# Retention chunks tiled across the batches, integer passes in PSUM, one weight load later

## The chip, the cores and the metric

The kernel runs on one core of one Trainium2 chip. The metric is device time in microseconds (us), the median of three runs. The profile is one execution of its own, read with the chip's hardware profiler.

## The reference

Three layers follow one another; all inputs are float32 but the dense layer's weights `w_in` and `w_out`, which are float64.

```python
# 1. retention: q, k, v of 4 batches x 8 heads x 576 x 64
scores = scale * np.matmul(q, k.transpose(0, 1, 3, 2))
Dmat = np.where(rel >= 0, gamma[:, None, None] ** rel[None, :, :], 0.0)
x = np.matmul(scores * Dmat[None], v)            # then laid out as 2304 tokens x 512
# 2. dense layer, 512 -> 2048 -> 512
h = x @ w_in
x = (np.maximum(h, 0.0) + np.log1p(np.exp(-np.abs(h)))) @ w_out
# 3. routed layer: 8 experts, the best two of each token
noisy = x @ w_gate + np.log1p(np.exp(x @ w_noise)) * noise
for e in range(E):
    for k in range(2):
        h = np.maximum(x[mask] @ w1[e], 0.0)
        out[mask] += top2_w[mask, k, None] * (h @ w2[e])
```

## The kernel before

**Retention** is done in chunks of 96 positions, six to a sequence, 24 in all. A chunk's own part is a masked product: Q is the product of its k and q (`att_qk`, L218), multiplied by the mask on VectorE (L222), and V is that times v (`att_av`, L258). What comes from earlier chunks of the same sequence goes through a state: K sums the scaled k times v (`att_kv`, L235) onto the last state (L238), and a later chunk adds state times scaled q to its V (L254). S scales q and k on GpSimd (`att_scale`, L206 and L209). Chunks are numbered batch by batch, so the first chunk of a sequence, which needs no state, is every sixth, and a tile of four chunks (384 tokens) holds four neighbours in one sequence. ScalarE and VectorE write a chunk's result as a high and a low float16 half (L264, L265).

**The dense layer** goes tile by tile, six tiles of 16 steps. A step is twelve products of the first layer (`g1`, L277), its relu and absolute value on ScalarE (L286, L287), the exp and ln for two steps together (L289, L290), a sum and a cast on VectorE (L291, L292), the low half on GpSimd for the first 24 steps (L294), and four steps later nine products of the second layer (`g2`, L308). High and low halves are multiplied three ways.

**Decoding.** The float64 weights of this layer come as 16 pieces of 1 MB, loaded in the order of a list (i: first layer, o: second). Each is turned into float32 by ScalarE and VectorE (`decode`, L135 to L140), and then into a high half on ScalarE (L146) and a low one on GpSimd (L147). Piece i0 serves the first two steps, i1 the next two, and so on. The third layer's weights are float32 and are split in the same way in 64 units, stored to DRAM (L321 to L335).

**The order of the work** at the beginning is a table, `START`: A loads a chunk, S, Q, K, V as above, L loads a piece, a decodes one, b splits it, g is a step, r loads what the router needs, W is warming of TensorE. From there on `at` hooks chunks and units to steps. A scheduler then sets the order on each engine from this and from its own estimates. Every engine, and the DMA queue on SyncE (SP), works its own list in order; the instruction at its head may wait for a semaphore and holds up those behind. Buffers are shared: two arrays `w1` and `w2` (in the traces w, in the orders below w_84 and w_85) hold first the pieces and all that belongs to retention, later the experts' weights. A ring with n places makes its n+1st writer wait for the first reader. Products L218, L235 and L258 share two PSUM tiles (pa), the first layer has two (pg), the second three (p2, also used by the first chunks), and a last bank (sm) serves the router.

**The routed layer** needs a schedule of blocks, made by VectorE in two parts, the first before the last tile is through. Then 41 blocks follow: a gather on GpSimd, a transpose by DMA (L621), the first product (L633), a transpose, the second product (L650), and an addition into the output. `weights(i, half)` loads 2 MB of an expert's weights, half 0 for the first product and half 1 for the second; `out_zero` writes zeros to the output beforehand (L350). The last tile's router waits for its own transposed rows (L394, L406).

Of the kernel before, what the change touches and what calls it, by code (L numbers as in the profile page):

```python
# [45 lines left out]
def consts():  # L46

    gamma = 1.0 - 2.0 ** (-5.0 - np.arange(H))
    i = np.arange(C)
    rel = i[None, :] - i[:, None]  # L50
    m = np.where(rel >= 0, gamma[:, None, None] ** np.maximum(rel, 0), 0.0) / np.sqrt(D)
    g = gamma.reshape(4, 2).T
    s = np.arange(S)
    cq = np.repeat(g[:, None, :, None] ** s, D, axis=1) / np.sqrt(D)
    ck = gamma[None, :] ** -s[:, None]
    return {
        "c_m": m.reshape(4, 2, C, C).transpose(2, 1, 0, 3).astype(np.float32),
        "c_q": cq.reshape(P, 4, NCB, C).transpose(2, 0, 1, 3).astype(np.float32),
        "c_k": ck.reshape(NCB, C, H).transpose(1, 0, 2).astype(np.float32),
    }  # L60


def chunks(q, k, v):


    def cols(a):
        return a.reshape(B, 4, 2, NCB, C, D).transpose(0, 3, 2, 5, 1, 4).reshape(B * NCB, P, 4, C)

    def rows(a):
        return a.reshape(B, H, NCB, C, D).transpose(0, 2, 3, 1, 4).reshape(B * NCB, C, H, D)  # L70

    return {"qk": np.stack([cols(q), cols(k)], axis=2), "kv": np.stack([rows(k), rows(v)], axis=2)}
# [3 lines left out]
def body(ctx, tc, ins, out):  # L76
# [49 lines left out]
    def decode(d):  # L126
# [10 lines left out]
        nc.scalar.activation(w[:, :, 0], u[:, :, 1], AF.Copy, bias=2.0 ** -14 - 0.5, scale=2.0 ** -13)  # L137
        nc.vector.scalar_tensor_tensor(out=A, in0=w[:, :, 1], scalar=3, in1=w[:, :, 0],
                                       op0=ALU.logical_shift_left, op1=ALU.bitwise_or)
        nc.vector.scalar_tensor_tensor(out=A, in0=w[:, :, 1], scalar=-2 ** 31, in1=A,  # L140
                                       op0=ALU.bitwise_and, op1=ALU.bitwise_or)
# [37 lines left out]

    cm = view(1, 12288, [2, 4 * C], F32, C).rearrange("p a (b c) -> p a b c", b=4)  # L180
# [3 lines left out]
    def att_load(c):  # L184
        cc = c % NCB
# [4 lines left out]
        kv = ap.tile([C, 2, H, D], F32, name="kv", bufs=3)  # L190
        nc.sync.dma_start(out=kv, in_=ins["kv"][c])
        if c == 0:
            nc.sync.dma_start(out=ck, in_=ins["c_k"])
        if 0 < c < NCB:
            CQ[c] = view(1, 15616 + (c - 1) * 1536, [4, C], F32)
            nc.sync.dma_start(out=CQ[c], in_=ins["c_q"][c])
        LD[c] = (qk, kv)

    def att_scale(c):
        qk, kv = LD[c]  # L200
        cc = c % NCB
        qs = ks = None
        e = nc.vector if c < 1 else nc.gpsimd
        if cc < NCB - 1:
            ks = ring("ks", 1, 23296, [H, D], F32, 2, C)
            e.tensor_tensor(out=ks, in0=kv[:, 0], in1=ck[:, cc, :, None].to_broadcast([C, H, D]), op=ALU.mult)  # L206
        if cc:
            qs = ring("qs", 1, 27392, [4, C], F32, 2)
            e.tensor_tensor(out=qs, in0=qk[:, 0], in1=CQ[cc], op=ALU.mult)  # L209
        SC[c] = (qs, ks)  # L210

    def att_qk(c):

        qk, kv = LD[c]
        pa = [ps1.tile([C, 4, C], F32, tag="pa", name="pa", bufs=2) for g in range(2)]
# [9 lines left out]
    def att_kv(c, tag="pa"):  # L225
        (qk, kv), (qs, ks) = LD[c], SC[c]
        cc = c % NCB
        if cc == NCB - 1:
            return
        pst = ps.tile([P, 4, D], F32, tag=tag, name="pst", bufs=3) if tag == "p2" else \  # L230
            ps1.tile([P, 4, D], F32, tag="pa", name="pst", bufs=2)

        for j in range(4):
            for r in range(2):
                nc.tensor.matmul(pst[ROW[r], j], lhsT=ks[:, 2 * j + r], rhs=kv[:, 1, 2 * j + r], start=True, stop=True)  # L235
        st = ring("st", 1, 30464, [4, D], F32, 2)
# [4 lines left out]
        ST[c + 1] = st  # L241

    def att_av(c, tag="pa"):
        (qk, kv), (qs, ks), a = LD.pop(c), SC.pop(c), AA.pop(c)
        cc = c % NCB
# [10 lines left out]
        for j in range(4):  # L256
            for r in range(2):
                nc.tensor.matmul(px[ROW[r], j, :], lhsT=kv[:, 1, 2 * j + r], rhs=a[r][:, j], start=n < 2, stop=n >= last - 1)  # L258
# [99 lines left out]
    def route_load():  # L358
        nc.sync.dma_start(out=table.rearrange("(p a c) f -> p a (c f)", p=P, c=17),
                          in_=init.rearrange("p (o c) f -> p o (c f)", o=1).to_broadcast([P, NCOL // 17, 68]))  # L360
        nc.sync.dma_start(out=noise, in_=ins["moe2_noise"].rearrange("(j p) e -> p j e", p=P))
# [12 lines left out]
    nc.gpsimd.iota(tok, pattern=[[P, NB]], base=0, channel_multiplier=1)  # L374
    ones = rt.tile([P, P], F16, name="ones")
# [64 lines left out]
    def ranks(t):  # L440
# [28 lines left out]
        nc.vector.tensor_copy(tb[:, :, :, 1], tkb)  # L469
# [249 lines left out]
    for n in range(64):  # L719
# [9 lines left out]
        W6 W16 A0 L A1 S0 Q0 K0 A2 L S1 V0 Q1 K1 A3 L a V1 S2 Q2 K2 L V2 S3 a b Q3 K3 L V3 a b L g g  # L729
        a A4 b L g g a S4 b L g Q4 a K4 b A5 L g g V4 a b L g S5 g Q5 a b L g K5 A6 g a V5 b L g g S6  # L730
        a b L g Q6 g a K6 b A7 L g V6 g a b S7 L g g Q7 a b K7 A8 L g V7 g a b L S8 g g Q8 a b g K8 g a V8 b r
        g g g g b
# [3 lines left out]
    def step():  # L736
# [11 lines left out]
        if u == (2, NTILE * NS - 5 - DELTA):  # L748
            LIST["a"] = schedule(True, NBA)
            for i in range(PA):  # L750
                if i == 0:
                    weights(i, 0)
                    weights(i, 1)
# [8 lines left out]
    for s in START:  # L762
# [6 lines left out]
        else:  # L769
            c = int(s[1:])  # L770
            f = {"A": att_load, "S": att_scale, "Q": att_qk, "K": att_kv, "V": att_av, "W": warm}[s[0]]
            f(c, "p2") if s[0] in "KV" and c < 4 else f(c)
# [12 lines left out]
    for i in range(NMAIN + LAG):  # L785
# [11 lines left out]
        if i < NMAIN:  # L797
            e1(i)
            if i + 1 < NMAIN:
# [45 lines left out]
```

## Time and profile before

| what | value |
|---|---|
| median of three runs | 975.64 us (971.98 to 978.98) |
| the profiled execution's own time | 975.07 us |
| its span, first to last instruction | 973.1 us |
| mean granted TensorE clock | 0.966 |
| TensorE busy | 914.0 us (94%) |
| VectorE, ScalarE, GpSimd busy | 408.0, 373.5, 282.2 us |

[...] A busy time is an average over stages with different limits, so each stage has to be read by itself. GpSimd's durations are rough. A row's bracket says how long the engine stood idle before it and what ended that.

### The profile page before, as it was taken

The numbers are of one execution on the slowest core, as the hardware profiler recorded it, in microseconds if no ns is written. First come the engines' busy times: TensorE is split into PE (matmuls) and PEld (weight loads), VectorE is DVE, ScalarE is ACT, GpSimd is POOL, SyncE is SP. The second block draws the span as 40 slices with busy tenths as digits, with TensorE's granted clock in tenths as the row PEclk, the third lists the DMA queues.
The fourth block names the chain that finished last, engine by engine and source line by source line (L and its number), as shares of the span: only waits on it lengthen the run. The fifth ranks groups of instructions, "written<-read, shape, count | busy, mean of one in ns | idle before, by whom it ended". The sixth has DMA issues, their size and how long they took to land. (4 is left out here: it accounts for less than half of the span.)

```text
span 973.1 us, 17382 instructions
## 1 busy us (share of the span) xinstructions
PE 914.0 (94%) x5690; PEld 470.3 (48%) x5690; DVE 408.0 (42%) x725; ACT 373.5 (38%) x585; POOL 282.2 (29%) x237
## 2 busy tenths in 40 slices
PE   8876799999989999999998999999999999999796
PEld 7543355555545555555543444444444444444342
DVE  4599956766477687634443411111111111111010
ACT  2767565566367566445432111211112111111111
POOL 3387932521310140020130422223223222322112
PEclk7799789999999999999999999999999999999899
DMA  9857769999999999300248698899999999999973
GB/s 309 283 162 248 173 247 288 305 357 278 317 329 349 335 354 339 100 1 7 60 172 202 94 164 133 141 262 195 224 135 203 218 224 181 209 272 210 197 166 53
DMA packets 221427, 206.69 MB, mean 212 GB/s; under 512 B 159360, under 2 KB 169216, under 8 KB 219296
## 3 DMA queue, kind: packets, MB, share of 16 engines
q1 hardware_dynamic: 211008, 185.29, 69.8%
q0 software_dynamic: 10336, 20.27, 11.7%
q8 instruction: 54, 0.88, 0.4%
q14 instruction: 29, 0.24, 0.1%
HBM read 245.70 MB, written 54.20 MB: 308 GB/s over the span
## 5 line engine op out<-in xcount | busy, mean ns | idle before, releaser
L633 PE MATMUL ph<-w,xt 128*128 x984 | 223.5, 383 | 9.1 <-DMA w<-wsc 8.0
L650 PE MATMUL py<-w,ht 128*128 x984 | 218.9, 379 | 1.7 <-DMA w<-wsc 1.7
L308 PE MATMUL p<-w,g 128*128 128x512 f16 x864 | 205.0, 385 | 7.2 <-POOL w L147 5.5
L277 PE MATMUL pg<-x,wi 128*128 128x384 f16 x1152 | 207.5, 331 | 3.5 <-POOL wi L147 2.0
L638 DVE SCALAR_TENSOR_TENSOR hr<-ph,hr 128x512 f16<-128x512 f32 x82 | 56.7, 691 | 358.8 <-ACT hr L637 336.0
L633 PEld LDWEIGHTS <-xt 128*128 128x128 f16 x984 | 96.8, 99 | 127.1 <-issue 15.2
L277 PEld LDWEIGHTS <-wi 128*128 128x128 f16 x1152 | 112.9, 99 | 89.8 <-issue 7.4
L650 PEld LDWEIGHTS <-ht 128*128 128x128 f16 x984 | 96.2, 98 | 118.0 <-issue 2.1
L662 POOL DMA_INDIRECT out_dram<-y,ti x41 | 65.3, 1593 | 298.7 <-ACT y L661 277.4
L308 PEld LDWEIGHTS <-g 128*128 128x128 f16 x864 | 81.5, 99 | 100.7 <-issue 12.2
L637 ACT ACTIVATE hr<-ph 128x512 f16<-128x512 f32 x82 | 49.0, 597 | 166.4 <-PE ph L633 160.2
L661 ACT ACTIVATE y<-py,ti 128x512 f32<-128x512 f32 x41 | 28.2, 688 | 195.6 <-PE py L650 191.1
L331 DVE SCALAR_TENSOR_TENSOR w<-w 128x1024 f16<-128x1024 f32 x64 | 81.4, 1277 | 51.8 <-ACT w L330 43.1
L330 ACT ACTIVATE w<-w 128x1024 f16<-128x1024 f32 x64 | 67.3, 1055 | 52.1 <-DMA w<-in_moe_w_dram 32.0
L291 DVE SCALAR_TENSOR_TENSOR r<-a,r 128x768 f32<-128x768 f32 x48 | 56.0, 1166 | 70.8 <-ACT a L290 70.4
L286 ACT ACTIVATE r<-pg 128x384 f32<-128x384 f32 x96 | 46.8, 487 | 99.8 <-PE pg L277 91.8
L478 POOL DMA_INDIRECT table<-tb,pos x36 | 42.7, 1186 | 120.0 <-DVE pos L463 95.3
L206 POOL TENSOR_TENSOR w<-kv,w 96x512 f32<-96x512 f32 x19 | 26.8, 1410 | 94.2 <-PE pst L235 66.4
L617 POOL DMA_INDIRECT xr<-X,ti x41 | 43.6, 1063 | 24.3 <-DMA xt<-xr 11.7
L209 POOL TENSOR_TENSOR w<-qk,w 128x384 f32<-128x384 f32 x20 | 28.0, 1398 | 69.6 <-PE px L254 37.2
L287 ACT ACTIVATE a<-pg 128x384 f32<-128x384 f32 x96 | 46.7, 487 | 0.0
L290 ACT ACTIVATE a<-a 128x768 f32<-128x768 f32 x48 | 40.5, 843 | 1.0
(126 smaller groups left out, 647.1 us busy)
## 6 DMA issues: line engine op xcount, KB each, us to landing
w<-wsc SPq DMA_DIRECT2D x78, 2048.0 KB
w<-in_moe_w_dram SPq DMA_DIRECT2D x64, 512.0 KB
wsc<-w SPq DMA_DIRECT2D x64, 512.0 KB
qk<-in_qk_dram SPq DMA_DIRECT2D x24, 384.0 KB
kv<-in_kv_dram SPq DMA_DIRECT2D x24, 384.0 KB
w<-in_moe_w_in_dram SPq DMA_DIRECT2D x8, 1024.0 KB
w<-in_moe_w_out_dram SPq DMA_DIRECT2D x8, 1024.0 KB
out_dram<-zero SPq DMA_DIRECT2D x1, 4608.0 KB
```

The costliest lines, as they stand in the source:

```text
L277: nc.tensor.matmul(pg, lhsT=wi[:, a, k, f * P:(f + 1) * P], rhs=x[:, b, k, :], start=n == 0, stop=n == 11)
L286: nc.scalar.activation(r[:, i], pg, AF.Relu, scale=S_G / sx)
L287: nc.scalar.activation(a[:, i], pg, AF.Abs)
L291: nc.vector.scalar_tensor_tensor(out=r, in0=a, scalar=S_G, in1=r, op0=ALU.mult, op1=ALU.add)
L308: nc.tensor.matmul(PG[t, j], lhsT=g[:, a, f % 2, j * P:(j + 1) * P], rhs=wo[b][:, f, :], start=f == 0 and a + b == 0, stop=f == NFB - 1 an ...
L330: nc.scalar.activation(h[:, 0], t, AF.Copy, scale=s)
L331: nc.vector.scalar_tensor_tensor(out=h[:, 1], in0=t, scalar=s, in1=h[:, 0], op0=ALU.mult, op1=ALU.subtract)
L633: M1[i].append(nc.tensor.matmul(ph, lhsT=xt[:, a * 4 + k, :], rhs=AR[0][:, ds(r * 8192 + (b * 4096 + k * 1024 + n * 512), 512)], start=m = ...
L637: LAST["act"] = nc.scalar.activation(hr[:, 0, n * 512:(n + 1) * 512], ph, AF.Relu)
L638: nc.vector.scalar_tensor_tensor(out=hr[:, 1, n * 512:(n + 1) * 512], in0=ph, scalar=0.0, in1=hr[:, 0, n * 512:(n + 1) * 512], op0=ALU.max ...
L650: M2[i].append(nc.tensor.matmul(py, lhsT=ht[:, a * 8 + c, :], rhs=AR[1][:, ds(r * 8192 + (b * 4096 + c * 512), 512)], start=len(M2[i]) == ...
L662: LAST["pool"] = nc.gpsimd.indirect_dma_start(out=out[:, :], out_offset=bass.IndirectOffsetOnAxis(ap=ti[:, 1:2], axis=0), in_=y[:, :], in_ ...
```

## The change

1. Chunks are numbered across the batches: chunk c is part c // 4 of batch c % 4. A tile now holds the same part of the four sequences, the first tile holds four first parts, and a state is used four chunks later. The inputs are laid out in this order on the host, the noise too, and a second token table `tok2` gives each row's place in the output.
2. The first four chunks load q, k for Q and v only; their k for the state comes with a new letter B, into free parts of `w1` and `w2`, and S and K of these chunks stand later. Q of chunks 1 and 3 uses the pg tiles.
3. In `decode` the low words go to a PSUM tile of 512 columns in the bank sm, one tile for all; a piece is done in two halves, and both integer passes read that tile.
4. `START` is rewritten.
5. `weights(0, 1)` moves from the schedule's end to behind the first block's first product.

```diff
{DIFF}
```

How the queues move at three places follows, in the order of the instructions and without any time. GpSimd at its first pieces of work, before (L206 and L209 scale k and q, L147 is the low part of a piece, L294 that of the hidden layer):

```order
L206 TENSOR_TENSOR w_85<-kv,w_85 96x512
L209 TENSOR_TENSOR w_85<-qk,w_85 128x384
L206 TENSOR_TENSOR w_85<-kv,w_85 96x512
L209 TENSOR_TENSOR w_85<-qk,w_85 128x384
L147 TENSOR_TENSOR wi<-w_85,wi 128x4x256
L206 TENSOR_TENSOR w_85<-kv,w_85 96x512
L209 TENSOR_TENSOR w_85<-qk,w_85 128x384
L147 TENSOR_TENSOR wi<-w_85,wi 128x4x256 x2
L294 TENSOR_TENSOR g<-r,g 128x768
```

And now (L222 and L225 scale, L153 is the low part, L309 that of the hidden layer):

```order
L153 TENSOR_TENSOR wi<-w_85,wi 128x4x256
L222 TENSOR_TENSOR w_85<-w_84,w_85 96x512 x4
L153 TENSOR_TENSOR wi<-w_85,wi 128x4x256
L309 TENSOR_TENSOR g<-r,g 128x768
L153 TENSOR_TENSOR wi<-w_85,wi 128x4x256
L153 TENSOR_TENSOR w_85<-w_85,w_84 128x1024
L309 TENSOR_TENSOR g<-r,g 128x768
L222 TENSOR_TENSOR w_85<-kv,w_85 96x512
L225 TENSOR_TENSOR w_85<-qk,w_85 128x384
```

The first piece's low part stands first; the four k are scaled in a row between it and the second piece's low part, and no q is scaled until the fifth chunk.

VectorE in the middle of the decoding, before (L138 and L140 are the two passes on a whole piece, L222 the mask product, L291 and L292 the hidden layer's sum and cast):

```order
L138 SCALAR_TENSOR_TENSOR w_85<-w_84 128x1024
L140 SCALAR_TENSOR_TENSOR w_85<-w_84,w_85 128x1024
L138 SCALAR_TENSOR_TENSOR w_85<-w_84 128x1024
L222 TENSOR_TENSOR a<-pa,w_85 96x384 x2
L140 SCALAR_TENSOR_TENSOR w_85<-w_84,w_85 128x1024
L238 TENSOR_TENSOR w_85<-w_85,pst 128x256
L291 SCALAR_TENSOR_TENSOR r<-a,r 128x768
```

And now (L144 and L146 on half a piece each, L238, L306 and L307 for the others):

```order
L146 SCALAR_TENSOR_TENSOR w_85<-w_84,low 128x512
L144 SCALAR_TENSOR_TENSOR low<-w_84,low 128x512
L146 SCALAR_TENSOR_TENSOR w_85<-w_84,low 128x512
L144 SCALAR_TENSOR_TENSOR low<-w_84,low 128x512
L146 SCALAR_TENSOR_TENSOR w_85<-w_84,low 128x512
L280 SCALAR_TENSOR_TENSOR x_595<-px,x_595 128x4x96
L306 SCALAR_TENSOR_TENSOR r<-a,r 128x768
L144 SCALAR_TENSOR_TENSOR low<-w_84,low 128x512
L307 CAST g<-r 128x768
L146 SCALAR_TENSOR_TENSOR w_85<-w_84,low 128x512
```

Four shorter passes stand for two long ones, each with the tile `low` as an operand, and the sum and the cast of the hidden layer come between the passes of one half.

SP at the beginning of the routed layer, before (L605 loads expert weights, L621 transposes gathered rows, L394 the router's rows, L396 stores these):

```order
L605 DMA w_84<-wsc 128x8192
L605 ISA
L605 REGISTER_ALU
L605 ISA
L605 DMA w_85<-wsc 128x8192
L621 DMA_TRANSPOSE xt<-xr 128x8x128 x3
L394 DMA_TRANSPOSE x2t<-rows 128x8x128
L621 DMA_TRANSPOSE xt<-xr 128x8x128
L396 DMA X_88<-rows 128x1024
```

And now (L622, L638, L411, L413; L658 transposes the first product's result):

```order
L622 DMA w_84<-wsc 128x8192
L638 DMA_TRANSPOSE xt<-xr 128x8x128 x4
L411 DMA_TRANSPOSE x2t<-rows 128x8x128
L413 DMA X_88<-rows 128x1024
L411 DMA_TRANSPOSE x2t<-rows 128x8x128
L413 DMA X_88<-rows 128x1024
L411 DMA_TRANSPOSE x2t<-rows 128x8x128
L413 DMA X_88<-rows 128x1024
L638 DMA_TRANSPOSE xt<-xr 128x8x128
L658 DMA_TRANSPOSE ht<-hr 128x16x128
```

Only one load of expert weights is left ahead of the transposes, four gathered transposes stand ahead of the router's first, and the second load has gone behind L658.

## Rows read from the trace of the kernel before

**Rows 1.** Busy: stretch, length; PE, PEld, VectorE, ScalarE, GpSimd; clock, DMA share, GB/s.
```profile
42.67:138.21 95.54, 72.67 (x555) 40.44 (x555) 86.34 (x62) 64.93 (x89) 70.78 (x33) 0.89 0.65 199
138.21:250.00 111.79, 109.40 (x859) 61.62 (x858) 77.89 (x135) 69.59 (x112) 31.38 (x19) 0.98 0.97 315
```
**Rows 2.** Timeline of ScalarE: start, duration, instruction; evictions, relus, the last high part.
```profile
10.18 0.49 ACT L264 ACTIVATE x<-px 128x384 f16<-128x384 f32 x1 [8.07 <-PE px L258]
...
38.78 0.51 ACT L286 ACTIVATE r<-pg 128x384 f32<-128x384 f32 x1
...
42.67 0.54 ACT L286 ACTIVATE r<-pg 128x384 f32<-128x384 f32 x1
...
122.12 1.06 ACT L146 ACTIVATE w<-w 128x1024 f16<-128x1024 f32 x1 [4.18 <-DVE w L140]
...
138.21 0.47 ACT L286 ACTIVATE r<-pg 128x384 f32<-128x384 f32 x1
```

**Rows 3.** Groups of VectorE from 42.67 to 138.21: busy, mean ns, idle before.
```profile
L140 DVE SCALAR_TENSOR_TENSOR w<-w,w 128x1024 int32<-128x1024 int32 x12 | 26.7, 2227 | 0.2
L138 DVE SCALAR_TENSOR_TENSOR w<-w 128x1024 int32<-128x1024 int32 x12 | 26.3, 2189 | 0.1
L291 DVE SCALAR_TENSOR_TENSOR r<-a,r 128x768 f32<-128x768 f32 x7 | 16.0, 2291 | 2.9 <-ACT a L290 2.8
L292 DVE CAST g<-r 128x768 f16<-128x768 f32 x7 | 6.3, 902 | 0.1
```

**Rows 4.** VectorE lines over the whole run: duration min/median/max in ns.
```profile
L138 DVE SCALAR_TENSOR_TENSOR w<-w x16: 1206/1482/5333, 12.7 to 116.0; 128x1024 int32<-128x1024 int32 x16
...
L222 DVE TENSOR_TENSOR a<-pa,w x48: 540/544/556, 8.2 to 424.2; 96x384 f32<-96x384 f32 x48
...
L265 DVE SCALAR_TENSOR_TENSOR x<-px,x x24: 543/550/559, 10.7 to 432.6; 128x384 f16<-128x384 f32 x24
...
L391 DVE SCALAR_TENSOR_TENSOR w<-p,w x15: 680/684/693, 150.6 to 462.4; 128x512 f16<-128x512 f32 x15
```

**Rows 5.** Timeline of GpSimd, VectorE and TensorE around 100 us.
```profile
99.69 3.10 POOL L147 TENSOR_TENSOR w<-w,w 128x1024 f16<-128x1024 f32 x1
...
100.73 3.14 DVE L138 SCALAR_TENSOR_TENSOR w<-w 128x1024 int32<-128x1024 int32 x1
...
103.80 1.01 DVE L222 TENSOR_TENSOR a<-pa,w 96x384 f32<-96x384 f32 x2
...
104.44 0.80 PE L235 MATMUL pst<-kv,w 96*64 96x64 f32 x10 [3.92 <-issue]
```

**Rows 6.** Groups of ScalarE from 42.67 to 138.21.
```profile
L135 ACT ACTIVATE w<-w 128x1024 f32<-128x1024 f32 x12 | 13.9, 1158 | 0.0
...
L146 ACT ACTIVATE w<-w 128x1024 f16<-128x1024 f32 x8 | 8.5, 1064 | 9.9 <-DVE w L140 9.9
...
L286 ACT ACTIVATE r<-pg 128x384 f32<-128x384 f32 x14 | 6.9, 492 | 5.4 <-PE pg L277 5.4
L290 ACT ACTIVATE a<-a 128x768 f32<-128x768 f32 x7 | 6.0, 851 | 0.0
```

**Rows 7.** GpSimd's subtraction L147 over the whole run: duration min/median/max in ns.
```profile
L147 POOL TENSOR_TENSOR w<-w,w x8: 2114/2132/3220, 49.5 to 123.3; 128x1024 f16<-128x1024 f32 x8
```

**Rows 8.** Timeline: GpSimd at the fourth chunk, TensorE at the first step.
```profile
23.35 1.04 POOL L206 TENSOR_TENSOR w<-kv,w 96x512 f32<-96x512 f32 x1 [1.29 <-DMA kv<-in_kv_dram]
...
31.65 0.48 PE L277 MATMUL pg<-x,wi 128*128 128x384 f16 x1 [0.58 <-ACT x L264]
```

**Rows 9.** Timeline of SP: the load behind the zeroing, the fourth gathered transpose.
```profile
246.08 11.17 SPq L187 DMA_DIRECT2D qk<-in_qk_dram  x1
...
522.16 1.23 SPq L621 DMA_TRANSPOSE xt<-xr  x1
```

**Rows 10.** Waits of TensorE from 490 to 600 us: total, times, longest.
```profile
PE lg L406 <- DMA x2t<-rows: 4.4, 2, 2.6
```

**Rows 11.** Busy time by stretch (columns as in rows 1) while the first expert weights load.
```profile
506.00:509.00 3.00, 3.00 (x19) 1.66 (x17) 0.00 (x0) 0.08 (x1) 0.20 (x2) 1.00 1.02 431
```

More of the change, by code (lines that the diff above doesn't have):

```diff
@@ L135, in decode @@
         nc.scalar.activation(h, h, AF.Copy, scale=2.0 ** -111)
[L137 to L141, printed above, removed]
+        for n in range(2):
+            r = slice(n * 512, (n + 1) * 512)
+            low = ps.tile([P, 512], I32, tag="sm", name="low", bufs=1)
+            nc.scalar.activation(low, u[:, r, 1], AF.Copy, bias=2.0 ** -14 - 0.5, scale=2.0 ** -13)
+            nc.vector.scalar_tensor_tensor(out=low, in0=w[:, r, 1], scalar=3, in1=low,
+                                           op0=ALU.logical_shift_left, op1=ALU.bitwise_or)
+            nc.vector.scalar_tensor_tensor(out=A[:, r], in0=w[:, r, 1], scalar=-2 ** 31, in1=low,
+                                           op0=ALU.bitwise_and, op1=ALU.bitwise_or)
         return f
@@ L189, in att_load, with att_load_k, att_qk @@
             nc.sync.dma_start(out=cm, in_=ins["c_m"])
[L190 to L191 removed]
+        if cc:
+            kv = ap.tile([C, 2, H, D], F32, name="kv", bufs=3)
+            nc.sync.dma_start(out=kv, in_=ins["kv"][c])
+            k, v = kv[:, 0], kv[:, 1]
+        else:
+            k, v = (ring(("kv", h), h, 40960, [H, D], F32, B, C) for h in range(2))
+            nc.sync.dma_start(out=v, in_=ins["kv"][c, :, 1])
         if c == 0:
             nc.sync.dma_start(out=ck, in_=ins["c_k"])
[L194 to L197, printed above, removed]
+        if cc and c % B == 0:
+            CQ[cc] = ring("cq", 1, 15616, [4, C], F32, 3)
+            nc.sync.dma_start(out=CQ[cc], in_=ins["c_q"][cc])
+        LD[c] = (qk, k, v)
+    def att_load_k(c):
+        nc.sync.dma_start(out=LD[c][1], in_=ins["kv"][c, :, 0])
     def att_scale(c):
[L200 to L201 removed]
+        qk, k, v = LD[c]
+        cc = c // B
         qs = ks = None
[L203 removed]
+        e = nc.gpsimd
         if cc < NCB - 1:
[L205 to L206 removed]
+            ks = ring("ks", 1, 20224, [H, D], F32, 2, C)
+            e.tensor_tensor(out=ks, in0=k, in1=ck[:, cc, :, None].to_broadcast([C, H, D]), op=ALU.mult)
         if cc:
[L208 removed]
+            qs = ring("qs", 1, 24320, [4, C], F32, 2)
             e.tensor_tensor(out=qs, in0=qk[:, 0], in1=CQ[cc], op=ALU.mult)
         SC[c] = (qs, ks)
[L212 to L215 removed]
+    def att_qk(c, tag="pa"):
+        qk = LD[c][0]
+        pa = [ps1.tile([C, 4, C], F32, tag=tag, name="pa", bufs=2) for g in range(2)]
         for j in range(4):
@@ L257, in att_av @@
             for r in range(2):
-                nc.tensor.matmul(px[ROW[r], j, :], lhsT=kv[:, 1, 2 * j + r], rhs=a[r][:, j], start=n < 2, stop=n >= last - 1)
+                nc.tensor.matmul(px[ROW[r], j, :], lhsT=v[:, 2 * j + r], rhs=a[r][:, j], start=n < 2, stop=n >= last - 1)
                 n += 1
@@ L374, in body @@
     nc.gpsimd.iota(tok, pattern=[[P, NB]], base=0, channel_multiplier=1)
+    tok2 = rt.tile([P, NB], I32, name="tok2")
     ones = rt.tile([P, P], F16, name="ones")
@@ L752, in step @@
                     weights(i, 0)
-                    weights(i, 1)
                 prep(i)
@@ L798, in body @@
             e1(i)
+            if i == 0:
+                weights(i, 1)
             if i + 1 < NMAIN:
```

45 lines of the change are left out of this document (25 added, 20 removed).

## Prediction

> **What bounds the kernel now.** I read the busy times by stretch first, then what each engine does in the stretch that loses most, then the few places where TensorE stands still.
>
> From the fourth first-layer step, whose relu starts at 42.67 us, to the seventeenth, at 138.21 us [rows 2], 95.5 us pass. TensorE is busy in 72.67 of them, at a granted clock of 0.89; VectorE in 86.34. In the next 112 us TensorE is busy 109.40 and loses 2.4 [rows 1]. So the loss that can be won back lies before 138 us, and there VectorE is the fullest engine. The reader should ask what fills it. The two integer passes of the decoding (L138, L140), twelve of each, take 26.3 and 26.7 us, a mean of 2.19 and 2.23 us [rows 3], while the shortest L138 of the run takes 1.206 us and the longest 5.333 [rows 4]. The products L222 and evictions L265, which read one operand in PSUM, never leave 540 to 559 ns in all 48 and 24 cases [rows 4], though they run in the same stretch. The passes with both operands in SBUF stretch whenever GpSimd is in a subtraction: at 99.69 GpSimd starts one of 3.10 us, at 100.73 VectorE starts an L138 that lasts 3.14, the products L222 queued behind it start at 103.80, and TensorE has idled 3.92 us when their PSUM tile comes free [rows 5]. ScalarE pays too: of its L146 rows, 9.9 us of idle time end at a VectorE L140 [rows 6].
>
> **The change part by part.**
>
> *Start.* The four chunks of tile 0 become four first chunks. They need no scaled q, no state product, no state, and for V only v. Queued ahead of the fourth chunk now are four qk and kv (0.75 MB each), three c_q (0.19) and two weight pieces (1 MB each); after it, four qk and v (0.56 MB each) and one piece. The fourth chunk's k arrived at 23.35, where GpSimd waits for it, and the first step began at 31.65 [rows 8]. In the new order that step is held by its own piece instead. From the second eviction, about 11.8 (the first is at 10.18 [rows 2], the second chunk a product and an eviction behind): scale 1.16, two halves of 0.61 + 2 x 0.68, four products of 0.54 between them, an eviction 0.49, high part 1.06, low part 2.11, and the first scaled k, 1.04, since the first K matmul stands ahead of the step: 23.8. (0.61 for a 512-wide ScalarE pass lies on the line through 492 ns for 384 and 851 for 768 [rows 6]; 0.68 is the 512-wide pass with a PSUM operand [rows 4]; 2.11 is GpSimd's subtraction at its shortest [rows 7].) Steps 1 and 2 took 31.65 to 38.78, 7.1 us at a low clock, steps 3 and 4 another 3.89 [rows 2]. Between step 2 and step 3 the new queue of GpSimd puts two scaled k and the second low part, 2 x 1.04 + 2.11 = 4.2. So the fourth relu starts at 23.8 + 7.1 + 4.2 + 3.9 = 39.0: **3.7 us earlier**, not the eight that the first step gains. Bounds: 0 if a k is late once more, 7 if the first two steps run at the full clock (3.9 for 7.1).
>
> *Decoding.* In the stretch between these two relus the new order has on ScalarE 11 scales (12.7), 25 halves (15.3), 13 high parts (13.8), 26 relu and abs (12.8), 14 exp and ln (11.9), and about 5.8 of evictions and weight casts: **72.3 us**. On VectorE 25 halves x 2 x 0.68 = 34.2, seven sums and casts at today's stretched 2.29 and 0.90 [rows 3], which stay in SBUF, 22.3, ten products 5.4, and 8.7 of evictions, states and weight splits: **70.6**, where it was busy 86.3. TensorE: its 72.67 at clock 0.89 are about 65 at full clock. GpSimd falls from 70.78 [rows 1] by what its subtractions are stretched, from 2.11 up to 3.22 [rows 7]. Nothing here is near 95.5 any more; ScalarE is the fullest. VectorE reached 90% of the old stretch, but two engines now hand each half to one another through one bank, so I take 86%. The wait that is added is ScalarE's, for VectorE's two passes before each second half; behind it in ScalarE's queue stand the relu and abs that free TensorE's first-layer tiles, so its lateness becomes TensorE's. With 86%, 72.3 / 0.86 is 84, **11.5 us earlier**. Bounds: 95% full gives 76 (19.5); nothing gained gives 0; less than that is a rival. The copies from the new token table sit in VectorE's queue behind a load that SP issues after the last piece; 1 MB at the 431 GB/s of [rows 11] is 2.4 us, so 0 to 4 of waiting, which I hold to lie inside the 14%.
>
> The price that the trace doesn't show is the half itself, a read and write in PSUM with a shift. The nearest rows, one PSUM operand, give 0.68; two of them cost 1.37 where one undisturbed 1024-wide pass cost 1.21, so a piece costs 2.74 for 2.41. [...]
>
> *Order later.* By the seventeenth step the new order has two state groups fewer and one K group more behind it: one group of sixteen small matmuls, 1.3 us at 0.80 for ten [rows 5], is done later: **-1.3**. The zeroing of the output moves ahead of the twelfth chunk's kv on SP's queue. Today SP's next load hangs 11.17 us behind it [rows 9]. I cost it at nothing, since DMA is 0.65 busy there and 0.97 where it stood before [rows 1], and since that kv is hooked to be scaled at step 22; without that cover it costs up to 11.
>
> *Second half.* The second 2 MB of expert weights move from ahead of the first three gathered transposes to behind the first block's. Today both loads run at 431 GB/s up to the transposes [rows 11]; the fourth transpose goes out at 522.16 only [rows 9], between two transposes that the router waits for, and TensorE loses 4.4 us to the router's inputs [rows 10]. 2 MB less is 4.9 us, so the fourth transpose is out ahead of these. I take **2 us**. Bounds: 5 (both waits and some clock), and -3 if the moved load is late for the second layer, now queued behind three blocks of the first.
>
> Sum: 3.7 + 11.5 - 1.3 + 2 = 15.9 off the profiled execution's 975.07 us (span 973.1; the median of the runs is 975.64, so nothing changes by going from one to the other): **959 us**.
>
> **Rivals.**
> (a) *The one bank becomes the bound.* A half holds it for 0.61 + 2 x 0.68 = 2.0 us if nobody is late, and the next can't begin before; 25 halves in 95.5 us leave 3.8 each. In seven halves a sum and a cast stand at the passes, 2.29 + 0.90 more: (18 x 2.0 + 7 x 5.2) = 72, which fits. If every half also waits for relus and products, to 4.5 us, the stretch is 112, 17 longer, and the kernel takes 988. It decides above 3.8. Against it: ScalarE's queue puts other work between the two halves of most pieces. [...] 15%.
> (b) *TensorE's own pace.* VectorE's lateness was all that held it; the stretch shrinks to 65 / 0.95 = 68, 27.5 gained: 943. For it: its longest waits end at VectorE or GpSimd. Against: ScalarE's 72.3. 12%.
> (c) *Given back.* From 138 us on DMA is 0.97 busy at 315 GB/s [rows 1]; if the splitting of expert weights is bound by it, what is won before 138 us is lost again, and the second half's 2 us and some 3 for the zeroing that leaves this stretch stay: 970. Against it: TensorE loses 2.4 of 112 there now, and the load per step is unchanged. 7%.
> (d) *The passes stay long*, since one operand and the last output are still in SBUF: the stretch grows by the fixed cost, 25 halves x 0.16 = 4.1: 975. The 48 products [rows 4] speak against it. [...] 6%.
> My forecast: 60%.
>
> **Numbers.** 959 is the forecast. Its own terms reach from 951 (a stretch of 76, the rest as taken) to 967 (a stretch of 92). The range 945 to 972 adds (c) and part of (b), and leaves out (a)'s and (d)'s upper parts and (b)'s end, under 2 in 10. One per cent, about what can be told from no change here, is 9.8 us: faster means below 965.9. Forecast 58 of its 60 and (b) 12: 0.70. (c), (d), nine of (a)'s fifteen and the rest: 0.24. Slower, (a)'s end: 0.06.
>
> **What the new profile would show.** The passes in PSUM at 0.6 to 0.75 us with hardly a spread, and GpSimd's subtractions near 2.1; if they spread to 3, (d). The fourth relu near 39 and the seventeenth near 123; ScalarE the fullest engine between. ScalarE's second half waiting for VectorE over 1.5 us a piece would be (a). TensorE's seventeenth step earlier but the same end would be (c). At the router, waits below 4.4 and the second layer's first matmul without a wait for weights. I am wrong if the fourth relu isn't earlier, or if the stretch stays above 92.

## The result

Both kernels ran seven times on one chip: 974.9 us before, 963.98 us after (960.32 to 968.59), a ratio of 0.9891 with a 95% interval of 0.986 to 0.9922. In six later runs, beside other kernels, the changed one took 963.99 us, a ratio of 0.9866 (0.9818 to 0.9915). So the change is worth 1.1 to 1.3%; the forecast was 959 with a range of 945 to 972. Medians here and below are of all runs; the ratios leave out the few runs in a slower state and are not quotients of these medians, so that the two needn't rank kernels alike.

The profiled execution took 963.04 us with a span of 961.3, at a mean granted clock of 0.98, a share of full speed. Its span is 11.8 us shorter. Where that was won and lost shows in a few marks of the two timelines:

| mark | before | after | earlier by |
|---|---|---|---|
| fourth first-layer relu | 42.67 | 36.97 | 5.7 |
| seventeenth | 138.21 | 123.85 | 14.4 |
| last (96th) | 509.10 | 489.85 | 19.3 |
| ScalarE's result y of the third routed block | 574.72 | 557.61 | 17.1 |
| the last block's y | 965.42 | 953.42 | 12.0 |

The change wins 19.3 us up to the routed layer, more than forecast, and gives 7.3 back in it.

Busy times by stretch, the two that answer to [rows 1] (same columns):

```profile
36.97:123.85 86.88, 74.08 (x587) 39.65 (x588) 59.95 (x95) 64.42 (x100) 53.52 (x34) 0.96 0.83 253
123.85:250.00 126.15, 125.52 (x1031) 71.58 (x1029) 93.30 (x161) 79.96 (x128) 36.86 (x26) 1.00 0.99 328
```

VectorE falls from 86.3 us to 60.0, GpSimd from 70.8 to 53.5, and the stretch from 95.5 to 86.9. TensorE, which lost 2.4 of 112 us in the next stretch, now loses 0.6 of 126. The relus that answer to [rows 2], on ScalarE's timeline:

```profile
26.41 0.49 ACT L301 ACTIVATE r<-pg 128x384 f32<-128x384 f32 x1 [3.90 <-PE pg L292]
...
36.97 0.48 ACT L301 ACTIVATE r<-pg 128x384 f32<-128x384 f32 x1
...
123.85 0.49 ACT L301 ACTIVATE r<-pg 128x384 f32<-128x384 f32 x1
```

VectorE's groups in the stretch, for [rows 3]: the two passes on halves (L144, L146), the sum and the cast.

```profile
L144 DVE SCALAR_TENSOR_TENSOR low<-w,low 128x512 int32<-128x512 int32 x26 | 18.0, 690 | 13.5 <-ACT low L143 12.7 <-DMA wg<-in_moe_w_gate_dram 0.7
L146 DVE SCALAR_TENSOR_TENSOR w<-w,low 128x512 int32<-128x512 int32 x26 | 17.8, 685 | 1.4
L306 DVE SCALAR_TENSOR_TENSOR r<-a,r 128x768 f32<-128x768 f32 x7 | 8.6, 1227 | 2.9 <-ACT a L305 2.9
L307 DVE CAST g<-r 128x768 f16<-128x768 f32 x7 | 6.4, 912 | 0.0
```

And the durations over the whole run, minimum, median and maximum in ns, for [rows 4, 7]: a pass, the decoding's subtraction on GpSimd (L153), and the hidden layer's (L309).

```profile
L144 DVE SCALAR_TENSOR_TENSOR low<-w,low x32: 675/696/701, 13.0 to 122.6; 128x512 int32<-128x512 int32 x32
```
```profile
L153 POOL TENSOR_TENSOR w<-w,w x8: 2122/2135/2812, 43.5 to 125.7; 128x1024 f16<-128x1024 f32 x8
```
```profile
L309 POOL TENSOR_TENSOR g<-r,g x12: 1639/1644/1650, 34.9 to 162.0; 128x768 f16<-128x768 f32 x12
```

The passes have lost their spread: 26 ns between the shortest and the longest, where the old one ran from 1206 to 5333. Now look at who waits in this stretch, TensorE first, then ScalarE (total, times, longest):

```profile
PE pg L292 <- POOL wi L153: 5.9, 5, 1.7
PE p L323 <- POOL w L153: 4.9, 5, 1.6
```
```profile
ACT r L301 <- PE pg L292: 14.0, 10, 3.0
ACT low L143 <- DVE w L146: 6.5, 5, 2.6
```

ScalarE waits for TensorE twice as long as for the bank. TensorE waits for the last link of the decoding chain, the low half that GpSimd subtracts. From 490 us on TensorE waits for this, in the place of [rows 10]:

```profile
PE ph L650 <- DMA w<-wsc: 10.2, 5, 6.3
PE ph L650 <- DVE hr L655: 3.6, 1, 3.6
PE py L667 <- DMA w<-wsc: 2.3, 2, 1.2
PE py L667 <- ACT y L678: 1.9, 2, 1.0
PE lg L423 <- DMA x2t<-rows: 1.3, 2, 1.1
```

The router's wait fell from 4.4 to 1.3 us. Two waits are new: one of 3.6 for an eviction on VectorE (hr), and two of about 1 for ScalarE's y.

### The profile page after: what moved, and what is told of

Same layout as the page of the kernel before. It is cut to its first block, busy times and chain, and to the rows that moved or that the text cites. A ratio compares the mean times of both kernels' runs of the same rounds, so it can differ in the third digit from the quotient of the medians.

```text
span 961.3 us, 17458 instructions
## 1 busy us (share of the span) xinstructions
PE 907.9 (94%) x5690; PEld 462.8 (48%) x5690; DVE 384.1 (40%) x756; ACT 375.1 (39%) x601; POOL 264.1 (27%) x238
## 5 line engine op out<-in xcount | busy, mean ns | idle before, releaser
L292 PE MATMUL pg<-x,wi 128*128 128x384 f16 x1152 | 209.3, 331 | 8.7 <-POOL wi L153 7.0
L323 PE MATMUL p<-w,g 128*128 128x512 f16 x864 | 201.3, 379 | 6.6 <-POOL w L153 4.9
L292 PEld LDWEIGHTS <-wi 128*128 128x128 f16 x1152 | 111.4, 99 | 94.3 <-POOL wi L153 9.3
L346 DVE SCALAR_TENSOR_TENSOR w<-w 128x1024 f16<-128x1024 f32 x64 | 84.8, 1329 | 39.7 <-ACT w L345 39.4
L306 DVE SCALAR_TENSOR_TENSOR r<-a,r 128x768 f32<-128x768 f32 x48 | 48.6, 1013 | 67.1 <-ACT a L305 66.8
L225 POOL TENSOR_TENSOR w<-qk,w 128x384 f32<-128x384 f32 x20 | 25.0, 1249 | 92.8 <-issue 53.5
L304 ACT ACTIVATE a<-a 128x768 f32<-128x768 f32 x48 | 40.4, 842 | 1.2
L305 ACT ACTIVATE a<-a 128x768 f32<-128x768 f32 x48 | 40.3, 841 | 1.0
```

The source lines that it names most:

```text
L292: nc.tensor.matmul(pg, lhsT=wi[:, a, k, f * P:(f + 1) * P], rhs=x[:, b, k, :], start=n == 0, stop=n == 11)
L306: nc.vector.scalar_tensor_tensor(out=r, in0=a, scalar=S_G, in1=r, op0=ALU.mult, op1=ALU.add)
L323: nc.tensor.matmul(PG[t, j], lhsT=g[:, a, f % 2, j * P:(j + 1) * P], rhs=wo[b][:, f, :], start=f == 0 and a + b == 0, stop=f == NFB - 1 an ...
L346: nc.vector.scalar_tensor_tensor(out=h[:, 1], in0=t, scalar=s, in1=h[:, 0], op0=ALU.mult, op1=ALU.subtract)
```

## The experiments

Twelve kernels ran, four to a chip, each four with their own runs of the kernel before. Ratios are to these, with 95% intervals.

| kernel | median us | ratio |
|---|---|---|
| 1 the new passes alone | 954.55 | 0.9816 (0.9759 to 0.9873) |
| 2 the whole change with the old passes | 980.92 | 1.0061 (1.0024 to 1.0097) |
| 3 the change, second load back | 961.26 | 0.9885 (0.9846 to 0.9923) |
| 4 the second load moved, nothing else | 978.42 | 1.005 (1.0012 to 1.0088) |
| 5 halves, but in SBUF | 981.17 | 1.0057 (1.002 to 1.0095) |
| 6 the new passes and the moved load | 961.18 | 0.9809 (0.9746 to 0.9872) |
| 7 the new passes, low products last | 955.25 | 0.9774 (0.9725 to 0.9823) |
| 8 the whole change again | 963.99 | 0.9866 (0.9818 to 0.9915) |
| 9 the change, first k's later | 974.99 | 0.9998 (0.9964 to 1.0032) |
| 10 the change, evictions first | 958.32 | 0.9841 (0.9789 to 0.9893) |
| 11 the new passes alone again | 956.45 | 0.9828 (0.9775 to 0.9882) |
| 12 three edits together | 969.41 | 0.9935 (0.9897 to 0.9974) |

1 to 4, 5 to 8 and 9 to 12 share a chip. In nearly every kernel the scheduler places the other work anew, so an edit can move more than its own lines; where it does, it is said.

**1 and 11. The new passes alone.** The kernel before with only this:

```diff
-        nc.scalar.activation(w[:, :, 0], u[:, :, 1], ...)
-        ... two passes on 1024 columns, low words in w[:, :, 0]
+        for n in range(2):
+            low = ps.tile([P, 512], I32, tag="sm", name="low", bufs=1)
+            ... the same on 512 columns each, low words in low
```

> The kernel before, with the new passes alone (halves, low words in the PSUM bank); chunk order, first tile, table and weight loads as before. The scheduler moves other work around the new instructions, so only the kernel's table is the same. Theory A (the passes carry the middle: free of GpSimd they shrink from 2.2 us to 0.69 each): the passes are 0.68 to 0.70 without spread, GpSimd's subtractions near 2.2, the stretch from fourth to seventeenth relu falls from 95.5 to about 87 and the total to 965 to 968. Theory B (the new order carries it, since it puts fewer products and states between the first steps): the passes are short too, but the stretch stays above 92 and the total is 972 to 976, because the state groups and q scalings still stand in the way.

> The kernel before with the new passes alone, once more beside variants of the whole change on one chip. By its first runs 0.976 to 0.987 of the kernel before, about 954 to 958 where that takes 974; if the whole change is as good and the difference was the chip, this comes out at 0.986 to 0.992.

By its medians it is faster than the whole change, both times, 954.55 and 956.45 us against 963.98 and 963.99. The passes alone and the whole change never stood on one chip, though, and their intervals overlap at the edge; the nearest pairs that did share one, 1 with 3 and 6 with 8, follow below. The passes (L141, L143 here) are as expected, and from the fourth relu to the seventeenth it needs 81.75 us in the first profile and 80.41 in the second:

```profile
38.94:120.69 81.75, 69.08 (x554) 37.97 (x554) 57.07 (x86) 63.58 (x98) 54.04 (x32) 0.98 0.78 246
```
```profile
40.77:121.18 80.41, 67.45 (x554) 37.43 (x554) 58.76 (x86) 63.39 (x98) 53.44 (x32) 1.00 0.78 242
```

The fourth relu stands at 38.94 and 40.77, 3.7 and 1.9 us before that of the kernel before, with the old order of the chunks. Theory B, that the order carries the gain, is out; Theory A holds and was too modest: the whole is worth 1.7 to 1.8%.

**2. The change with the old passes.** The diff of 1, taken the other way, on the changed kernel.

> The changed kernel, with the old two passes on a whole piece in SBUF; all else changed, the rest of the order as the scheduler then makes it. Theory A: the passes are stretched to 2 us and more again, fourth relu at about 38 (two to three passes late), the stretch to the seventeenth 92 to 96, total 971 to 975. Theory B: stretch 87 to 89 as in the changed kernel, total 963 to 967.

Slower than the kernel before. Its relus show Theory A's figures: the fourth at 37.93, the seventeenth at 133.42, 95.5 us between them. The passes on whole pieces take 1770 and 2520 ns on average, in the groups from 30 to 140 us:

```profile
L143 DVE SCALAR_TENSOR_TENSOR w<-w,w 128x1024 int32<-128x1024 int32 x14 | 35.3, 2520 | 0.2
L141 DVE SCALAR_TENSOR_TENSOR w<-w 128x1024 int32<-128x1024 int32 x14 | 24.8, 1770 | 9.2 <-POOL w L222 3.8 <-POOL w L219 2.9 <-ACT w L140 1.9
```

The total lies above Theory A's 971 to 975: what is left of the change without the passes is a loss of 0.6%.

**5. Halves, but in SBUF.** Kernel 1 with one line changed:

```diff
-            low = ps.tile([P, 512], I32, tag="sm", name="low", bufs=1)
+            low = w[:, r, 0]
```

> The kernel before with the passes in halves, but the low words in place in SBUF, as they were; it differs from the kernel that has only the new passes (954.6 us) in the bank alone. Theory E (the PSUM operand is what helps: passes with both operands in SBUF wait for GpSimd's subtractions): the 512-wide passes are 0.6 us at their shortest and 2 to 4 at their longest, mean above 1.0, and the total is 968 to 978. Rival F (shorter passes are enough: the queue behind a pass moves on sooner, whatever the pass reads): mean 0.65 to 0.8, total 953 to 960.

Theory E, and more strongly than expected. The groups of VectorE between 30 and 135 us, and the same line over the whole run:

```profile
L143 DVE SCALAR_TENSOR_TENSOR w<-w 128x512 int32<-128x512 int32 x28 | 39.1, 1417 | 0.5
L141 DVE SCALAR_TENSOR_TENSOR w<-w 128x512 int32<-128x512 int32 x28 | 31.6, 1150 | 4.8 <-ACT w L140 4.8
```
```profile
L143 DVE SCALAR_TENSOR_TENSOR w<-w x32: 677/693/3606, 15.1 to 123.7; 128x512 int32<-128x512 int32 x32
```

At its shortest a half takes 0.677 us in SBUF and 0.672 in PSUM; the mean in SBUF is 1.42 and the longest 3.606, where none of the 32 in PSUM took more than 0.689 (kernel 1, L143). The bank makes the whole difference, 981 us against 955, and the halves are what it costs to have it.

**3 and 4. The moved load.** In 3 it goes back in the changed kernel, in 4 it is moved in the kernel before:

```diff
                 if i == 0:
                     weights(i, 0)
+                    weights(i, 1)        # 3; 4 takes this line out
...
             e1(i)
-            if i == 0:
-                weights(i, 1)            # 3; 4 puts these in
```

> The changed kernel, with the second 2 MB of the first expert loaded ahead of the gathered transposes again. In the changed kernel 19.3 us are won at the last relu, 23 at the first block's end, and 12.0 at the end of the span. Theory C (the moved load costs later what it gives at the router: the first blocks wait, 23 falls to 17 by the third block): with it back the router waits are near 4.4 us again, but the third block is 18 to 20 us ahead of the kernel before, and the total is 960 to 963. Theory D (the move is worth its 2 us, and what is lost later is lost to something else, the transfers of the routed layer): total 965 to 967, third block 15 to 16 ahead. In both, if the routed layer is held by its transfers, the end moves by less than the third block does.

> The kernel before, with that one load moved and nothing else. Theory C: router waits fall from 4.4 us to about 1.3, VectorE's and ScalarE's waits in the first blocks take 3.6 and 1.9 in their place, total 974 to 977. Theory D: total 971 to 973.

Alone the move is slower, by 0.5%: not Theory D, and a little above C. With the load back, the waits of the router and the first blocks are the old ones, the first two rows below, from 500 to 600 us; with the load moved in the kernel before, they are those of the changed kernel, the other three:

```profile
PE lg L423 <- DMA x2t<-rows: 4.4, 2, 2.6
PE ph L650 <- DVE scb L519: 1.2, 1, 1.2
```
```profile
PE ph L633 <- DVE hr L638: 3.6, 1, 3.6
PE py L650 <- ACT y L661: 1.9, 2, 1.0
...
PE lg L406 <- DMA x2t<-rows: 1.0, 1, 1.0
```

How far a mark lies ahead of the kernel before (negative: earlier), in all profiles:

| kernel | load | last relu | third block's y | last y |
|---|---|---|---|---|
| after | moved | -19.3 | -17.1 | -12.0 |
| 8 | moved | -15.9 | -13.5 | -13.8 |
| 6 | moved | -20.4 | -17.4 | -13.9 |
| 2 | moved | +1.4 | +5.3 | +8.4 |
| 4 | moved | +0.7 | +3.0 | +11.2 |
| 9 | moved | -2.8 | +0.1 | -0.4 |
| 10 | moved, evictions first | -17.6 | -18.6 | -18.1 |
| 1 | old place | -20.3 | -20.0 | -20.8 |
| 11 | old place | -17.4 | -18.0 | -19.6 |
| 7 | old place | -22.9 | -22.8 | -22.8 |
| 3 | old place | -12.7 | -13.0 | -12.9 |
| 5 | old place | +3.9 | +4.0 | +1.2 |
| 12 | old place | -9.6 | -10.1 | -2.1 |

From the last relu to the third block, six kernels with the moved load lose 2.1 to 3.9 us, and those with the load in its old place 0.3 at most, or win up to 0.6. That is the same in each, and it is the move. After the third block it isn't so clear: 5.1 more in after, 0.3 won in 8, the same kernel, and 8.0 lost in 12 without the move. Of the seven with the moved load five lose 0.5 to 8.2 us there, of the six others two lose 2.8 and 8.0. What is mostly waited for there are expert weights, 6.7 to 15.5 us in all, and how much differs between executions of one kernel. I leave open what decides it. Of Theory C the mechanism holds, counted from the last relu; kernel 3 had won 6.5 us less there than after, so its third block is 13.0 ahead and not 18. Its total of 961 settles nothing, for the ratio, 0.9885, is that of the changed kernel.

**10. The evictions first.** Why a load makes TensorE wait for VectorE can be read from two timelines of the changed kernel. TensorE's next block can't begin, since its PSUM tile is not free:

```profile
517.49 6.74 PE L650 MATMUL ph<-w,xt 128*128 x24 [3.56 <-DVE hr L655]
...
535.63 2.75 PE L667 MATMUL py<-w,ht 128*128 x12 [1.05 <-ACT y L678]
```
```profile
508.49 0.68 DVE L655 SCALAR_TENSOR_TENSOR hr<-ph,hr 128x512 f16<-128x512 f32 x1
516.76 0.68 DVE L655 SCALAR_TENSOR_TENSOR hr<-ph,hr 128x512 f16<-128x512 f32 x1
```

Between these two evictions VectorE does the router's and the schedule's small operations without a gap; in kernel 3 an eviction stands in their midst (519.01, 522.34, 528.16). Kernel 4 has the same wait with the load alone moved, so it is the scheduler's answer to the load's new place. So:

```diff
-            nc.vector.scalar_tensor_tensor(out=hr[:, 1, ...
+            with tc.high_priority() if i < 4 else ExitStack():
+                nc.vector.scalar_tensor_tensor(out=hr[:, 1, ...
```

> The changed kernel with VectorE's evictions of the first four routed blocks ahead of the schedule's small operations, where they are ready. In every kernel with the moved load TensorE waits 3.6 us there for one such eviction, and twice about 1 us for ScalarE's y; without the move neither shows. Theory K (these waits are the scheduler's answer to the later load, and are what the move loses of its 3 us at the router): the 3.6 us wait falls below 1 us, the third block's y comes 2 to 3 us earlier against the last relu, total 960 to 963. Rival L (the schedule ends later by what it lets pass, and the next block waits for it instead): the wait for the eviction turns into one for the schedule's results of the same size, total 963 to 967.

Theory K for the eviction: its wait is gone, and 1.0 us is won up to the third block where 2.1 and 2.4 were lost. The total of 958.32 lies below the expected 960 to 963, with an interval that overlaps the changed kernel's. Rival L's wait for the schedule didn't come. ScalarE's y is waited for as before, 2.1 us, so Theory K doesn't hold for that part. What is new is the wait that the prediction had as its lower bound, for the moved weights themselves (from 490 to 600 us):

```profile
PE py L668 <- ACT y L679: 2.1, 2, 1.3
PE lg L423 <- DMA x2t<-rows: 1.6, 2, 1.3
PE py L668 <- DMA w<-wsc: 1.3, 1, 1.3
```

**6 and 8. What the order costs.** 6 is kernel 1 with the moved load; so it is the change without its chunk order, first tile and table. 8 is the change itself.

> The kernel before with the new passes and the moved load, so the changed kernel without its chunk order, first tile and table. If parts add up (load alone +4.9, passes alone -19, by the runs so far): 957 to 960, and the kernel with everything is 4 to 7 slower in the same runs, so the new order costs that. If instead the load explains all that the whole change loses against the passes alone: 962 to 966, as the kernel with everything. In the profile: VectorE's hr wait of 3.6 us and two waits of about 1 us for ScalarE's y in the first blocks, as in every kernel with the moved load.

> The changed kernel once more, beside the others on one chip: 962 to 966 by its first seven runs, a ratio of 0.986 to 0.992 to the kernel before. If its end was pulled by the execution profiled, the routed layer's waits for weights (12.5 us there) differ here; if they belong to the moved load they are above 10 again, against 8.0 in the kernel with the passes alone.

6 is 0.6% below 8 by the ratios, 0.3% by the medians, as if parts added up, though the intervals overlap. The same step shows between 1 and 3 (0.7%), which share a chip too, and in the time of the seventeenth relu: 123.85, 127.47, 124.09 and 125.65 in the four kernels with the new order and the new passes (after, 8, 3, 10), 120.69, 119.60, 120.56 and 121.18 in those with the old order (1, 6, 7, 11). With the new passes the order costs 4.8 us there, on the average of four and four. Where, two stretches at full clock tell, kernel 6 and kernel 10, each from its fourth to its seventeenth relu:

```profile
39.16:119.60 80.44, 67.45 (x554) 37.43 (x554) 58.79 (x86) 63.57 (x98) 53.43 (x32) 1.00 0.79 244
```
```profile
39.90:125.65 85.75, 71.19 (x587) 38.68 (x588) 60.30 (x95) 64.34 (x100) 53.51 (x34) 1.00 0.81 253
```

33 more products of TensorE, 32 of them small ones of retention, 3.7 us, and 1.6 more of idle time. Ahead of the fourth relu the new order has 48 products fewer, but wins only 1.0 us on the average of the same four and four; the granted clock up to there was 0.79 to 0.87 with it and 0.83 to 0.91 without. The first relu comes earlier, at 26.4 to 30.0 against 32.0 to 34.0, and the next three take 10.5 to 11.0 us for 6.9 to 7.3, because the scalings and state products of the first four chunks stand between them: in the changed kernel 54 state products take 2.5 us there, and TensorE waits 1.9 us for GpSimd, which scales two k ahead of the second piece's low half. Expected of 8 was also a wait for weights above 10; it is 9.6.

With the old passes the order doesn't cost this. In kernel 2 the seventeenth relu stands at 133.42, against 138.21, 136.63 and 140.73 in the kernels with the old passes and the old order (before, 4, 5), one execution each; and of the 0.6% that kernel 2 loses, the load alone costs 0.5% (kernel 4).

**9. The first k's later.** Meant to take these out of the first steps:

```diff
-        W6 W16 A0 A1 L A2 Q0 Q1 V0 A3 V1 L B0 a Q2 Q3 V2 B1 V3 b L a B2 B3 L S0 S1 a L
-        g b g a L b K0 S2 g K1 S3 g a L b g K2 g g K3
-        A4 a L b S4 g Q4 g a L b K4 g V4 g g
+        W6 W16 A0 A1 L A2 Q0 Q1 V0 A3 V1 L a Q2 Q3 V2 V3 b L a L b g g a B0 B1 L S0 K0 S1 g K1
+        B2 B3 b g a L b S2 K2 g S3 K3 g a L b g g
+        A4 a L b S4 g Q4 g a L b K4 g V4 g
```

> The changed kernel with another table: the k of the first four chunks are loaded after the fourth piece, and scaled and summed after the second piece's low half, so that no state product and no scaling stands between the first two steps. So far the kernels with the new order need 10.5 us from the first relu to the fourth, those with the old one 6.9, and 86 to 87 against 80 to 82 from the fourth to the seventeenth. Theory I (the state products and scalings of the first four chunks, put off into the steps, are what the new order costs): first to fourth relu 6 to 8 us, the seventeenth 4 to 7 us earlier than in the changed kernel, total 957 to 960. Rival J (they only move: the same 64 products and 4.2 us of GpSimd are paid a few steps later): first to fourth relu shorter, the seventeenth within 2 us of the changed kernel's, total 962 to 966.

Neither. The first relu came at 24.95 and the fourth at 35.27, still 10.3 later, and the seventeenth at 129.59. The edit took the work out of the way only from the first relu to the second (2.4 us for 3.3). Between the second and the fourth TensorE still does two groups of state products, and GpSimd still scales three k, as its timeline shows:

```profile
31.00 2.04 POOL L222 TENSOR_TENSOR w<-w,w 96x512 f32<-96x512 f32 x2
33.65 1.10 POOL L222 TENSOR_TENSOR w<-w,w 96x512 f32<-96x512 f32 x1 [0.62 <-POOL w L222]
```

So the first steps are no test of Theory I. SP's timeline tells why the seventeenth relu is none either: the scheduler drew the zeroing of the output forward to 90.67, ahead of the last weight pieces, whose loads hang 15.35 us behind it.

```profile
90.67 0.57 SPq L365 DMA_DIRECT2D out_dram<-zero  x1
93.98 15.35 SPq L125 DMA_DIRECT2D w<-in_moe_w_out_dram  x2
```

From 100 to 120 us DMA is then full, and VectorE and ScalarE, the engines of the decoding, are busy 9.15 and 8.85 of 20 us, against 14.55 and 15.22 in the changed kernel:

```profile
100.00:120.00 20.00, 16.55 (x114) 9.04 (x115) 9.15 (x15) 8.85 (x16) 8.64 (x5) 0.88 1.05 326
```

**7. Low products last**, kernel 1 with TensorE's products in another sequence:

```diff
-        for k in range(KC):
-            for a, b in ((0, 0), (0, 1), (1, 0)):
+        for k, ab in [(k, ((0, 0), (0, 1))) for k in range(KC)] + [(k, ((1, 0),)) for k in range(KC)]:
+            for a, b in ab:
...
+        jab = ... [(j, ((0, 0), (1, 0))) for j in range(3)] + [(j, ((0, 1),)) for j in range(3)]
```

> The new passes alone, and the products that read a low half of the weights put last: in a first-layer step all eight with the high half before the four with the low one, in a second-layer step six of nine before three. Same products, same sums in another order. In the kernel with the passes alone TensorE waits 11.9 us for GpSimd's low halves between the fourth and seventeenth relu. Theory G (this last link of the decoding chain holds TensorE there): these waits fall below 4 us, the stretch from 81.8 to 73 to 77, total 945 to 951. Rival H (the chain as a whole, ScalarE's queue above all, sets the pace, so that the wait only moves to the high half): stretch 79 to 82, waits for ScalarE's high half in place of GpSimd's low one, total 952 to 956.

The waits for GpSimd's low halves fall from 11.9 to 6.1 us, the stretch only to 79.65, of which 69.85 are busy at a clock of 0.98:

```profile
PE p L313 <- POOL w L150: 4.8, 5, 2.0
PE px L257 <- DVE a L225: 2.1, 1, 2.1
PE pg L280 <- ACT a L290: 1.5, 1, 1.5
PE pg L280 <- POOL wi L150: 1.3, 2, 0.7
PE p L313 <- ACT w L149: 0.9, 1, 0.9
```

The stretch and the total are Rival H's, but not its mechanism: the high half is waited for only 0.9 us. Of Theory G half holds: the link held TensorE for some 6 us, and with it eased other waits of 1 to 2 us show. With 955.25 us and 0.9774 it has the lowest ratio, but against 1 and 6 the difference is smaller than the intervals.

**12. Three edits together**: the table of 9, the load of 3, the products of 7, all on the changed kernel.

> The changed kernel with three edits: the table of the kernel with the later k, the second 2 MB of the first expert back ahead of the transposes, and low-half products last. If these three are what it loses or leaves (Theory I for the table), 950 to 953, faster than the passes alone; if the new order costs for another reason, as the rival J says, 956 to 960, no faster than the passes with low-half products last (955).

Neither: 969.41. It has 9's fault, the zeroing stands at 94.04, and it waits 15.5 us for expert weights. The kernels with the lowest ratios, 1, 6, 7 and 11, all keep the old order, though their intervals overlap that of 10.

## Why the prediction held, and where it didn't

**The start** (3.7 us, relu at 39.0): measured 36.97 in the profile, 40.53, 38.35 and 39.90 in three more executions with this order. The size is right, on average. Its cause is only half of it, and that the size fits is luck: the passes alone, with the old order, bring the relu to 38.94 to 40.91, and the new order alone, with the old passes, to 37.93 (kernel 2, one execution). The two don't add up: on top of the passes the order is worth some 1.0 us. The low clock that steps 1 and 2 were forecast at was 0.65 in the kernel before, from 31.65 to 38.78 us, and 1.00 in the two steps after them.

**The decoding** (84 us, bounds 76 to 95.5): 86.88, and 86.94, 85.74 and 85.75. The argument held: VectorE was filled by passes that stretched beside GpSimd, 2.19 and 2.23 us on average, and with a PSUM operand they took 0.690 and 0.685. The prediction's "whenever" says too much, though. Of the 24 passes in the old stretch 15 took 1.74 to 5.33 us, all beside work of GpSimd, three of them beside scalings alone. Nine took 1.21 to 1.23, and six of these started within 0.4 us of a subtraction on GpSimd: there it was the subtraction that was long, 2.49 to 3.23 us, where L294 took 1.64 at its shortest and L147 2.11. The half was taken at 0.61 and twice 0.68 and measured 0.635, 0.690 and 0.685. ScalarE's rows add up to 74.2 us, 72.3 were counted, 85% of the stretch where I took 86%. The profile's own busy time for it is 64.42, since neighbouring rows overlap by about 0.1 us (9.8 us over 100 rows); so 86% was right on the terms I used, and not a measure of a full engine. That the quotient fits is luck too, for ScalarE doesn't set the length: it waits 14.0 us for TensorE. What ends TensorE's waits, 10.8 us of them, is the chain up to GpSimd's low half, which I hadn't named. The sum and the cast, taken as stretched as before, fell to 1.23 us and stayed at 0.91.

**The order later** (-1.3): too small. By the seventeenth relu the order as a whole costs 4.8 us against the passes alone. I had counted the one state group that is put off and left out what the deferred groups take from the steps they fall into.

**The zeroing** (0): it went forward to 113.40 with a kv behind it, and TensorE doesn't wait for that, as the cover was reckoned:

```profile
113.40 0.58 SPq L365 DMA_DIRECT2D out_dram<-zero  x1
119.51 10.60 SPq L199 DMA_DIRECT2D kv<-in_kv_dram  x1
```

But it isn't the chunk order that moves it. It stands between 112 and 118 us in every kernel with passes in PSUM and an unchanged table, and between 233 and 245 in those without. And 0 was too low. From the seventeenth relu to the last, after wins 4.9 us; the other kernels with the zeroing between 112 and 118 (1, 3, 6, 7, 8, 10, 11) win between -1.4 and 5.2, 2.7 on average, and those with the late one (2, 4, 5) lose 1.4 to 6.2. That speaks for the 3 us that rival (c) had put on it, but doesn't show it: the three with the late zeroing are also those with the old passes, and no run moves the zeroing alone. Kernel 9 shows the other side, its price without cover.

**The second half** (+2, bounds -3 to 5): this step failed. The router's wait fell as forecast, by 3 us. I had priced what the load's place does to SP's queue, and taken the other engines' order as given. The new place changed VectorE's order too: an eviction went behind the schedule, 3.6 us, and the first blocks' y were met late, 1.9. From the last relu to the third block the move costs 2.1 us in the profile and 2.1 to 3.9 in six kernels; kernel 10 takes the eviction's part away.

**The sum.** Forecast 15.9 us; measured by the marks above 5.70 + 8.66 + 4.89 - 2.14 - 5.11 = 12.00 against the profiled execution before. Up to the last relu 19.25 was won where 13.9 was forecast; the second half came out 4.1 us below its +2, and 5.1 more was lost after it, for which the prediction had no term. Of these 5.1, 2.8 are waits for expert weights (12.5 us against 9.7 from 600 us on), 1.0 a wait for a transpose, and 1.4 TensorE's longer busy time for the same products. That the total fell so near the forecast is partly luck: errors of both signs stand against each other.

**The rivals.** (a) *One bank*: ScalarE waits 6.5 us for it in 25 halves, 0.26 each or half a us a piece, where over 1.5 a piece would have been its sign. Not it. (b) *TensorE's own pace*, a stretch of 68: no kernel came below 79.65; the chain holds. The 65 us that it rested on were too few as well: at full clock TensorE was busy 71.19 us in this order (kernel 10). (c) *Given back to DMA from 138 us on*: the opposite in that stretch; the 7.3 us that were given back later went to the first blocks and, as far as waits show, mostly to expert weights. (d) *The passes stay long*: 675 to 701 ns says no. The halves have a price, near the 0.16 us each that was reckoned: four passes cost 2.75 us where two undisturbed ones cost 2.41. The PSUM operand has none that shows: L143 at its shortest took 0.672 us with it (kernel 1) and 0.677 without (kernel 5). Kernel 5 pays the price of the halves without the bank and is 0.6% slower than before.

## What to carry to other kernels

Where VectorE's passes show a short minimum and a long mean while GpSimd works, try one operand in PSUM, even if the work must be cut in pieces for it: that alone was worth 1.7 to 1.8% here, and the same pieces in SBUF were a loss. When a transfer is moved in a kernel whose order a scheduler makes, read the new order of every engine near the place, not only of the queue it left. Test the parts of a bundled change one by one, though it wins: here one part gave more than the whole, by the medians.

## What the hardware showed unexpectedly

- A 512-wide integer pass takes, at its shortest, about the same time from SBUF alone (L141 0.674 us, L143 0.677, kernel 5) as with a PSUM operand (0.678 and 0.672, kernel 1). The medians are as near: 0.686 and 0.693 against 0.695 and 0.686.
- GpSimd gains as well: its subtraction of 768 columns ran from 1639 to 3031 ns, median 2480, in the kernel before, and takes 1639 to 1650 in the changed one, where VectorE's passes read PSUM. In the decoding its mean is 2226 ns before and 1645 after, 1920 with the halves in SBUF (kernel 5) and 2566 in the changed kernel with the old passes (kernel 2).
- With the same program in the first 120 us, the first relu came at 26.41, 29.99, 27.81 and 28.93 in four executions (after, 8, 3, 10), and the stretch to the seventeenth took 86.9 us at a granted clock of 0.96 (TensorE busy 74.1) and 85.7 at 0.98 and 1.00 (72.7 and 71.2). So single profiles of this kernel differ by some 3 us, which is why the small terms above rest on several.
